# Threshold attention and a gated MLP on one core: four heads in 32-row score tiles, q and k transposed by VectorE alone, batches cut into token halves

## The chip, the core and the metric

The kernel runs on one core of a Trainium2 chip. A core has a matrix engine (TensorE, PE in the profile; its weight loads are listed as PEld), a vector engine (VectorE, DVE), an activation engine (ScalarE, ACT), a general engine (GpSimd, POOL) and an engine that only issues transfers (SyncE, SP). Each runs its own queue in order, and they wait for each other through semaphores. Data moves between main memory and the on-chip memory SBUF by DMA; matmuls write to a second on-chip memory, PSUM, which has eight banks of 512 fp32 columns. The metric is device time in microseconds (us) for one launch, as the median of several runs.

## What is computed

```python
def _attn_ref(q, k, v, tau):                       # q, k, v: (8, 8, 576, 64), float32
    scale = 1.0 / np.sqrt(q.shape[-1])
    scores = scale * np.matmul(q, k.transpose(0, 1, 3, 2))
    thresh = np.max(scores, axis=-1, keepdims=True) - tau
    scores = np.where(scores >= thresh, scores, -1000000000.0)
    scores = scores - np.max(scores, axis=-1, keepdims=True)
    attn = np.exp(scores)
    attn = attn / (np.sum(attn, axis=-1, keepdims=True) + 1e-09)
    return np.matmul(attn, v)

def _moe_ref(x, w_in, w_out):                      # x: (4608, 512), w_in: (512, 2048), w_out: (2048, 512)
    h = x @ w_in
    return ((h * np.clip(h + 3.0, 0.0, 6.0) / 6.0) @ w_out)

# x = attention output as (batch * token, head * 64)
```

Eight batches of eight heads with 576 tokens each: scores in fp32, all scores below the row's maximum less tau rejected, a softmax over the rest, the product with v, and then two projections with a gate between them.

## The kernel before

**Slots.** The attention is cut into 144 slots. A quad is four heads of a batch (two pairs); a batch has two quads, and a quad has nine slots. Slots 0 to 3 are 128 query tokens each of the quad's first pair, 4 to 7 the same of its second pair, and slot 8 holds the last 64 tokens of both pairs. A slot is always two heads (`a` = 0 and 1) by 128 rows by 576 keys.

**What one slot does.** `scores(n)` (L300) multiplies q and k of two heads: each head's 64 dimensions are one half of the 128 partitions, so the two heads are two strips of TensorE, each with a 384- and a 192-column matmul (or 320 and 256). An fp32 matmul of the code shows in the trace as two records. `sm_max` (L315, DVE) copies the scores from PSUM to SBUF and takes the row maximum, one instruction for each head; `sm_bias` (L322, POOL) makes a bias of the maximum and tau; `sm_mask` (L327, ACT) and `sm_exp` (L332, ACT) reject, exponentiate and sum; `sm_recip` (L335, DVE) inverts the sum; `sm_norm` (L340, POOL) scales to bf16. The result P is then transposed, for most slots by a DMA (L348, issued by SP) and for some of the first 21 by nine TensorE transposes (L355) with a DVE copy (L356). `av_main` and `av_rest` (L364, L367) multiply P with v for 512 or 256 tokens or for the 64 last ones, and DVE copies the product out (xT at L375, xR at L385). From batch 2 on that is 256 tokens.

**Projections.** `mm1` (L393 with w_in) makes 512 columns of the first projection, which is called an item; relu goes to ACT (L412) or DVE (L414), and the gate to DVE (L427). `mm2_part` (L393 with w_out) is a quarter of a 128-token tile of the second projection, called a part; `mm2_out` (L446) copies a finished tile out on DVE, and `flush` sends it. There are 144 items and 144 parts. `todo1` and `todo2` are lists of what may be done; each slot from `N1` = 22 on takes one item, and every even one two parts. What is left after the last slot is done by `rest1` and `rest2`.

**q and k.** `load_quad` loads them. For the first two batches (`NB` = 2) TensorE transposes them (`main_pe` at L238, `transpose_rest` at L266 and L268), and DVE or ACT copies the result from PSUM. For the other six, loads of 32 numbers at a time put 32-dimension blocks below each other, and DVE's 32 x 32 transposes (L247 for q, L256 for k) finish the layout in SBUF.

**Order.** Nothing is scheduled automatically: each engine runs its instructions in the order in which the loop over slots writes them (L551). In slot n DVE does the maximum of slot n + 1, the reciprocal of n - 1, waiting copies, the product copy, relu, gate and transposes. TensorE does an item, the product, parts, and scores: one slot's scores (n + 2) in each of the slots 3 to 22, then, from slot 23 on, those of n + 3 and n + 2 in every odd slot. Scores lie in banks 0 to 5 (`score_col`), each head in three of them; the products use banks 2 and 5 in turn (`bank`), items bank 6 (HB) or 7, tiles of the second projection bank 7 (OB). `warm_up` issues transposes whose result nobody reads.

These lines say where a slot's scores stand and in which order a pair of slots is issued:

```python
def score_col(n, a):
    if n in (1, 2):
        return 1664 if a else 3200 if n == 1 else 128
    return (704 if first(n) else 128) + (0 if a else 1536)
...
elif n > N1 and n % 2:
    for m in (n + 3, n + 2):
        if m < len(queue):
            scores(m)
```

Of the kernel before, what the change touches and what calls it, by code (L numbers as in the profile page):

```python
# [20 lines left out]
def kernel(  # L21
# [17 lines left out]
    NQUAD = B * H // 4  # L39
    NSLOT = 9  # L40
    NB = 2
    N0 = 3
    N1 = 22
    N2 = 28
    HB, OB = 6, 7
    scale = 1.0 / math.sqrt(D)
# [3 lines left out]
    nat_pool = ctx.enter_context(tc.tile_pool(name="nat", bufs=3))  # L50
    v_pool = ctx.enter_context(tc.tile_pool(name="vp", bufs=2))
    qk_pool = ctx.enter_context(tc.tile_pool(name="qk", bufs=2))
# [3 lines left out]
    pt_pool = ctx.enter_context(tc.tile_pool(name="pt", bufs=3))  # L56
# [20 lines left out]
    loads = []  # L77
    casts = []
    vcasts = []
# [3 lines left out]
    def load_quad(quad):  # L83
        b, g = divmod(quad, 2)
        nat[quad] = (nat_pool.tile([P, 2 * S], F32, tag="nq", name="nq"),
                     nat_pool.tile([P, 2 * S], F32, tag="km", name="km"),
                     nat_pool.tile([P, 2 * D], F32, tag="kr", name="kr") if b < NB else None)
        nq, km, kr = nat[quad]

        def main(dst, src, n, a, order, by=nc.sync):  # L90
            by.dma_start(out=dst[:, 0:1024].rearrange("p (t h d) -> p t h d", h=4, t=4)[:, :, 2 * n + a, :],
                         in_=src[b, 4 * a + 2 * g + n, 0:512, :].rearrange(order, t=4))

        def blocks(dst, src, a, order, **sizes):
            rows = src[b, 4 * a + 2 * g:4 * a + 2 * g + 2].rearrange("n t d -> (n t) d")
            for j in range(2):
                c = 32 * (2 * a + j)
                nc.sync.dma_start(out=dst[c:c + 32].rearrange("p (k d) -> p k d", d=32) if len(sizes) == 1 else
                                  dst[c:c + 32].rearrange("p (t x d) -> p t x d", d=32, t=9),
                                  in_=rows[:, 32 * j:32 * j + 32].rearrange(order, **sizes))  # L100

        def load_k(n):
            if b < NB:
                for a in range(2):
                    main(km, k, n, a, "(p t) d -> p t d", by=nc.scalar if quad == n == 0 else nc.sync)
            else:
                blocks(km, k, n, "(x r t) d -> r t x d", r=32, t=9)

        def load_q(n):
            if b < NB:  # L110
                for a in range(2):
                    main(nq, q, n, a, "(t p) d -> p t d")
            else:
                blocks(nq, q, n, "(k r) d -> r k d", r=32)

        def rest():
            for dst, src in ((kr[:], k), (nq[:, 1024:1152], q)):
                for n in range(2):
                    by = nc.scalar if quad == 0 and src is k else nc.sync
                    by.dma_start(out=dst[64 * n:64 * n + 64, :].rearrange("p (h d) -> p h d", h=2),  # L120
                                 in_=src[b].rearrange("(a n) t d -> n a t d", a=2)[2 * g + n, :, 512:S, :].rearrange(
                                     "a p d -> p a d"))

        if b < NB:
            loads.extend((lambda: load_k(0), lambda: load_q(0), rest, lambda: load_k(1), lambda: load_q(1)))
        else:
            loads.extend((lambda: load_q(0), lambda: load_k(0), lambda: load_q(1), lambda: load_k(1)))

    def load_v(b):
        vm = v_pool.tile([P, H, 4 * D], BF16, tag="vm", name="vm")  # L130
        vr = vrs[b % 2]
        vsb[b] = (vm, vr)
        if b < NB:
            mains = [lambda h=h: nc.gpsimd.dma_start(
                out=vm[:, h:h + 4, :], in_=v[b, h:h + 4, 0:512, :].rearrange("h (p t) d -> p h (t d)", t=4))
                for h in range(0, H, 4)]
            rests = [lambda a=a: nc.gpsimd.dma_start(
                out=vr[a * 64:(a + 1) * 64, a, :, :],
                in_=v[b, 4 * a:4 * a + 4, 512:S, :].rearrange("h p d -> p h d")) for a in range(2)]
        else:  # L140
            def tokens(a, first, count):
                return v[b, 4 * a:4 * a + 4].rearrange("h (p t) d -> p h (t d)", t=9)[
                    :, :, first * D:(first + count) * D]

            mains = [lambda a=a, u=u, first=first: nc.gpsimd.dma_start(
                out=vm[64 * u:64 * u + 64, 4 * a:4 * a + 4, :], in_=tokens(a, first, 4))
                for a, u, first in ((0, 0, 0), (0, 1, 5), (1, 0, 5), (1, 1, 1))]
            rests = [lambda a=a: nc.gpsimd.dma_start(
                out=vr[a * 64:(a + 1) * 64, a, :, :], in_=tokens(a, 4 * (1 - a), 1)) for a in range(2)]
        vcasts.extend(mains + rests)  # L150
# [47 lines left out]


    gbuf = g_pool.tile([P, NI, 2 * S], BF16, name="g")  # L200

# [552 lines left out]
```

## Time and profile before

| | us |
|---|---|
| median of 3 runs (507.67 to 508.34) | 507.7 |
| the profiled execution | 506.6 |
| its span | 504.8 |
| maximum of slot 0 begins (DVE, L315) | 8.2 |
| maximum of slot 15 begins | 47.4 |
| maximum of slot 22 begins | 67.0 |
| maximum of slot 143 begins | 450.4 |
| last matmul begins to stream out, L680 | 497.8 |

The span is the time from the first to the last instruction of the program in the profiled execution; its time as a run is 1.8 us longer. Busy time is the sum of an engine's instructions without overlaps; in a row of a timeline the first number is the start, the second the length of a merged group and `xN` the number of records in it. Records of matmuls overlap, so from one matmul to the next it is the starts that count. A name after `<-` in brackets is what ended the idle time before.

### The profile page before, as it was taken

What the parts mean: (1) busy time and instruction counts of PE and PEld (TensorE: products, weight loads), DVE (VectorE), ACT (ScalarE), POOL (GpSimd) and SP (SyncE); (2) the same over time, 40 slices, a digit from 0 to 9 for tenths busy, and PEclk for the clock granted to TensorE, in tenths of its full rate; (3) what the DMA queues carried; (4) which work ended last, traced back from release to release, by engine and by line L of the source; (5) the groups of instructions that cost most, each with busy time, mean ns of one, the idle gap of its engine ahead of it and who ended that gap; (6) DMA issues with size and microseconds to landing.
All of it is one profiled execution on the core that took longest, in us unless ns stands there. A gap on an engine that the chain in (4) does not pass through costs nothing.

```text
span 504.8 us, 14628 instructions
## 1 busy us (share of the span) xinstructions
PE 497.2 (98%) x5496; PEld 343.8 (68%) x5496; DVE 443.3 (88%) x1151; ACT 444.3 (88%) x953; POOL 279.9 (55%) x509
## 2 busy tenths in 40 slices
PE   8999999999999999999999999999999999999997
PEld 7655567677766777777766777777766777767564
DVE  4788899999999999999999999999999999877261
ACT  4999999999999999999999999999999999986170
POOL 2777778756656555656556555656556555552000
PEclk9999999999999999999999999999999999999999
DMA  6999999999999999999999999999999996864122
GB/s 146 182 163 161 146 151 157 195 147 174 180 189 169 178 167 173 162 175 159 185 186 166 178 172 158 181 173 165 168 193 169 172 180 115 111 123 90 66 62 64
DMA packets 317814, 78.91 MB, mean 156 GB/s; under 512 B 300720, under 2 KB 313264, under 8 KB 317744
## 3 DMA queue, kind: packets, MB, share of 16 engines
q1 hardware_dynamic: 298784, 68.61, 88.3%
q0 software_dynamic: 17472, 8.92, 14.9%
q8 instruction: 43, 0.70, 0.6%
q10 hardware_dynamic: 1488, 0.46, 0.4%
q14 instruction: 27, 0.22, 0.2%
HBM read 36.70 MB, written 9.44 MB: 91 GB/s over the span
## 4 chain that ended last, share of the span: by engine, by line
PE 81%; DVE 5%; ACT 1%; issue 1%; DVEq 0%
PE ps L393 48%; PE ps L300 25%; PE ps L364 5%; DVE s L315 2%; PE ps L367 1%; DVE g L427 1%; DVE r L414 1%; PE ps L680 1%; ACT s L332 0%; ACT r L412 0%; PE ps L355 0%; DVE xT L375 0%; PE ps L238 0%; DVE kT L256 0%; DVE rinv L335 0%
## 5 line engine op out<-in xcount | busy, mean ns | idle before, releaser
L340 POOL TENSOR_SCALAR pn<-s,rinv 128x576 bf16<-128x576 f32 x288 | 211.6, 748 | 19.1 <-issue 4.6
L315 DVE TENSOR_SCALAR_CACHE_REDUCE s<-ps 128x576 f32<-128x576 f32 x288 | 204.7, 747 | 13.2 <-PE ps L300 6.5
L327 ACT ACTIVATE s<-s,bias 128x576 f32<-128x576 f32 x288 | 205.9, 764 | 3.6 <-POOL bias L322 3.2
L332 ACT ACTIVATE s<-s 128x576 f32<-128x576 f32 x288 | 192.5, 671 | 0.0
L300 PE MATMUL ps<-kT,qT 64*128 64x384 f32 (+7 forms) x1280 | 175.7, 419 | 2.3 <-DVE s L315 2.1
L300 PEld LDWEIGHTS ps<-kT,qT 64*128 64x128 f32 (+1 forms) x1280 | 104.1, 175 | 57.7 <-DVE s L315 10.2
L393 PE MATMUL ps<-xT,w_in_sb 128*64 128x256 bf16 (+1 forms) x1896 | 132.5, 274 | 0.6 <-DVE g L427 0.6
L393 PE MATMUL ps<-w_out_sb,g 128*64 128x512 bf16 (+1 forms) x1016 | 130.9, 379 | 0.0
L393 PEld LDWEIGHTS <-w_in_sb 128*64 128x64 bf16 (+1 forms) x1896 | 108.1, 109 | 31.6 <-issue 21.9
L322 POOL TENSOR_SCALAR bias<-m 128x2 f32<-128x2 f32 (+1 forms) x147 | 28.0, 190 | 161.2 <-DVE rinv L335 151.2
L427 DVE SCALAR_TENSOR_TENSOR g<-r,ps 128x512 bf16<-128x512 f32 x128 | 87.5, 685 | 11.8 <-ACT r L412 7.9
L393 PEld LDWEIGHTS <-g 128*64 128x64 bf16 (+1 forms) x1016 | 61.5, 109 | 48.3 <-issue 0.4
L412 ACT ACTIVATE r<-ps,three 128x512 f32<-128x512 f32 x81 | 55.5, 687 | 25.2 <-PE ps L393 23.2
L332 ACT ACTIVATION_READ_ACCUMULATOR s<-s 128x1 f32 x288 | 54.8, 190 | 0.0
L414 DVE TENSOR_SCALAR r<-ps 128x512 f32<-128x512 f32 x63 | 42.9, 680 | 0.0
L364 PE MATMUL ps<-pT,vm 128*64 128x256 bf16 (+1 forms) x480 | 38.5, 280 | 0.0
L364 PEld LDWEIGHTS <-vm 128*64 128x64 bf16 x736 | 32.7, 111 | 3.4 <-issue 1.4
L375 DVE CAST xT<-ps 128x256 bf16<-128x256 f32 (+1 forms) x60 | 26.1, 435 | 7.1 <-PE ps L367 7.1
L446 DVE TENSOR_SCALAR osb<-ps 128x512 f32<-128x512 f32 x31 | 20.9, 673 | 8.4 <-PE ps L393 8.4
L315 DVE DVE_READ_ACCUMULATOR s<-ps 128x1 f32 x288 | 23.8, 83 | 0.0
L335 DVE RECIPROCAL rinv<-rsum 128x2 f32<-128x2 f32 x144 | 23.0, 160 | 0.7 <-ACT s L332 0.6
L444 ACT ACTIVATE osb<-ps 128x512 f32<-128x512 f32 x4 | 2.4, 598 | 20.9 <-PE ps L393 14.6
(61 smaller groups left out, 249.6 us busy)
## 6 DMA issues: line engine op xcount, KB each, us to landing
out_dram<-osb SPq DMA_DIRECT2D x31, 256.0 KB, 3.0
nq<-in_q_dram SPq DMA_DIRECT2D x48, 144.0 KB, 4.4
km<-in_k_dram SPq DMA_DIRECT2D x48, 144.0 KB, 4.5
vm<-in_v_dram POOLq DMA_DIRECT2D x24, 128.0 KB, 4.3
nq<-in_q_dram SPq DMA_DIRECT2D x16, 128.0 KB, 4.5
w_in_sb<-in_moe_w_in_dram POOLq DMA_DIRECT2D x8, 256.0 KB, 4.9
w_out_sb<-in_moe_w_out_dram POOLq DMA_DIRECT2D x16, 128.0 KB, 4.5
pT<-pn SPq DMA_TRANSPOSE x117, 4.6
```

Of the source, the lines that this page charges most:

```text
L300: nc.tensor.matmul(ps_flat[rows, c0:c0 + w], qT_of(pair)[a * 64:(a + 1) * 64, q0:q0 + rows.stop - rows.start], kT_of(pair)[a * 64:(a + 1) ...
L315: nc.vector.tensor_scalar(out=sl.s[:, i, :], in0=ps_flat[:, c0:c0 + S], scalar1=1.0, scalar2=None, op0=Alu.mult, op1=Alu.max, accum_out=sl ...
L322: nc.gpsimd.tensor_scalar(out=sl.bias[:, of], in0=sl.m[:, of], scalar1=-scale, scalar2=tau, op0=Alu.mult, op1=Alu.add)
L327: nc.scalar.activation(out=s, in_=s, func=Act.Prelu, bias=sl.bias[:, i:i + 1], scale=scale, alpha=REJECT)
L332: nc.scalar.activation(out=s, in_=s, func=Act.Exp, accum_out=sl.rsum[:, i:i + 1])
L340: nc.gpsimd.tensor_scalar(out=pn[:, i, :], in0=sl.s[:, i, :], scalar1=sl.rinv[:, i:i + 1], scalar2=1.0, op0=Alu.mult, op1=Alu.mult)
L364: nc.tensor.matmul(pb[a * 64:(a + 1) * 64, :], vm[:, 4 * a + hp, c * D:(c + 1) * D], pT[:, 5 * a + c, cols], start=(c == 0), stop=False)
L375: return lambda: nc.vector.tensor_copy(out=xT[b][:, hp, c0:c0 + w], in_=pb)
L393: nc.tensor.matmul(out[c:c + w], lhsT[:, c:c + w], rhs, start=start, stop=stop)
L412: nc.scalar.activation(out=r, in_=hps, func=Act.Relu, bias=three[:])
L414: nc.vector.tensor_scalar(out=r, in0=hps, scalar1=3.0, scalar2=0.0, op0=Alu.add, op1=Alu.max)
L427: nc.vector.scalar_tensor_tensor(out=out, in0=r, scalar=6.0, in1=hps, op0=Alu.min, op1=Alu.mult)
```

## The change

Slots are laid out anew. A batch has 18 slots. Four heads (a quad) stand below each other in SBUF, each in 32 partitions, and the 64 dimensions are two halves `j` of 32 that lie side by side; a matmul has 32 rows, and two of them, one for each half, are accumulated. Two slots that follow each other have the same query tile and the two pairs of heads of a quad: slot `i` = 0 uses strips 0 and 1, slot `i` = 1 strips 2 and 3. The order within a batch is tokens 0 to 255 of both quads, the last 64 tokens of both quads, then tokens 256 to 511.

`burst(n)` issues both slots' scores together in eight steps, at the end of every even slot. The even slot's columns are cut into 128 and 448 (its 448 lie in bank 2 or 5), the odd slot's into 448 and 128, and the two 128-column pieces share a bank; a POOL instruction that does nothing (`relay`) keeps the odd slot's last piece behind the even slot's first.

q and k are transposed by DVE for all batches (`transpose_q`, `transpose_k`), k with rows of 18 tokens (4.6 KB) and q with rows of 64 numbers. The transposes of q and k for batch b + 1 stand in even slots of batch b, those of the first two quads and of quad 2 in slots 0 to 3, 5, 7, 9, 11 and 13, and quad 3's in 12, 14, 16, 18. v has one tile of five blocks for each head and is loaded in eight pieces. The weights are loaded in four and four transfers in place of eight and sixteen.

Products are of 256 tokens in every batch: chunk 0 in slots 8, 10, 12, 14 of the batch, the 64-token rest in 16, chunk 1 in 18, 20, 22, 24. Items are taken from slot 15 on, two parts in odd slots. P is transposed by TensorE only for slots 1, 3, 5, 7, 8, 9 and 11.

```diff
-    N0 = 3
-    N1 = 22
-    N2 = 28
+    NSLOT = 18
+    N1 = 15
...
+        if of:
+            src = k[b, 4 * g:4 * g + 4].rearrange("h (r t) d -> (h r) (t d)", r=R)
+            by.dma_start(out=dst, in_=src[:, t0 * D:t1 * D])
+            return
+        for c in range(4):
+            by.dma_start(out=dst[32 * c:32 * c + 32].rearrange("p (t d) -> p t d", d=D),
+                         in_=q[b, 4 * g + c].rearrange("(t r) d -> r t d", r=R)[:, t0:t1])
...
+    def transpose_q(quad, t0, t1):
+        rows = nat[quad][0][:].rearrange("p (t j w) -> p t j w", j=2, w=32)
+        nc.vector.transpose(out=qk_of(quad)[0][:].rearrange("p j (t w) -> p t j w", w=32)[:, t0:t1],
+                            in_=rows[:, t0:t1])
+    def transpose_k(quad, part):
+        first, e = ((0, 5), (10, 4))[part]
+        rows = nat[quad][1][:].rearrange("p (t j w) -> p j t w", j=2, w=32)
+        outs = qk_of(quad)[1]
+        for j in range(2):
+            for_u = rows[:, j, first:first + 2 * e].rearrange("p (u e) w -> p u e w", u=2)
...
+            nc.vector.transpose(out=o, in_=for_u)
...
+    for b in range(B):
+        for g, t in ((0, 0), (0, 1), (1, 0), (1, 1), (None, 4), (0, 2), (0, 3), (1, 2), (1, 3)):
+            for i in range(2):
+                sl = Slot()
+                sl.b, sl.g, sl.t, sl.i, sl.n = b, g, t, i, len(queue)
+                sl.on_chip = sl.n in (1, 3, 5, 7, 8, 9, 11)
+                queue.append(sl)
...
+    OWN = S - P
+    def score_col(n, a):
+        return (512 - OWN if n % 2 else 1024 - P) + 1536 * a
...
+    def burst(n):
+        steps = ((0, 0, P, 0), (1, 0, OWN, 0), (0, 0, P, 1), None,
+                 (0, P, OWN, 0), (1, 0, OWN, 1), (0, P, OWN, 1), (1, OWN, P, 0), (1, OWN, P, 1))
+        for step in steps:
+            if step is None:
+                relay = nc.gpsimd.nop()
+                behind(relay, mm)
+                continue
+            i, k0, w, j = step
+            sl = queue[n + i]
+            for a in range(2):
+                c = 32 * (2 * i + a)
...
+                    mm = nc.tensor.matmul(ps_flat[rows, c0:c0 + w],
+                                          qT[c:c + 32, j, q0:q0 + rows.stop - rows.start],
+                                          kT[c:c + 32, j, k0:k0 + w], start=(j == 0), stop=(j == 1))
+                    if (i, k0) == (1, OWN):
+                        behind(mm, relay)
...
+        at(products, n0 + 16, (b, None, None))
...
+        when = (7, 9, 11, 13) if quad == 2 else ((4, 6, 8, 10), (12, 14, 16, 18))[g]
+        for n, job in zip(when, (lambda quad=quad: transpose_k(quad, 0), lambda quad=quad: transpose_k(quad, 1),
+                                 lambda quad=quad: transpose_q(quad, 0, 8), lambda quad=quad: transpose_q(quad, 8, T))):
+            at(jobs, n0 + n, job)
+    at(jobs, 0, lambda: transpose_q(0, 4, 8))
+    for n, job in ((0, lambda: transpose_k(1, 0)), (1, lambda: transpose_k(1, 1)), (2, lambda: transpose_q(1, 0, 8)),
+                   (3, lambda: transpose_q(0, 8, T)), (5, lambda: transpose_q(1, 8, T))):
+        at(jobs, n, job)
...
+    for n, sl in enumerate(queue):
+        now = n
+        if n + 1 < len(queue):
+            sm_max(queue[n + 1])
+        if prev is not None:
+            sm_recip(prev)
+        for copy in waiting:
+            copy()
+        waiting = []
+        item = None
+        if todo1 and n >= N1:
+            item, then = todo1.pop(0)
+            h = mm1(item, 0 if n == len(queue) - 1 else OB if n > N1 and n % 2 == 0 and not pieces else HB)
+            todo2.extend(then)
+        multiply(n)
+        if item:
+            mm1_gate(item, h, mm1_relu(h, on_act=n % 2 == 1))
+        if n > 1 and queue[n - 2].on_chip:
+            waiting.append(pe_transpose(queue[n - 2]))
+        second()
+        for i in range(2):
+            sm_exp(sl, i)
...
+        for job in jobs.get(n, ()):
+            job()
+        if prev is not None:
+            sm_norm(prev)
+        if n % 2 == 0 and n + 2 < len(queue):
+            burst(n + 2)
+        if n < 3 or n == 6:
+            warm_up(6)
```

## The prediction

> **What bounds the kernel now.** First the page: its busy line, the chain, and the score line.
>
> ```profile
> span 504.8 us, 14628 instructions
> PE 497.2 (98%) x5496; PEld 343.8 (68%) x5496; DVE 443.3 (88%) x1151; ACT 444.3 (88%) x953; POOL 279.9 (55%) x509
> ...
> PE 81%; DVE 5%; ACT 1%; issue 1%; DVEq 0%
> ```
>
> The chain that ended last is TensorE for 81%. Busy time by stretch tells where that holds:
>
> ```profile
> 20.00:60.00 40.00, 38.72 (x309) 23.53 (x308) 35.39 (x101) 39.73 (x90) 30.98 (x55) 1.00 1.14 158
> ...
> 180.00:440.00 260.00, 260.00 (x3174) 183.58 (x3172) 249.57 (x653) 246.23 (x533) 150.12 (x271) 1.00 1.15 167
> 454.00:502.00 48.00, 47.28 (x340) 30.18 (x336) 21.77 (x37) 19.32 (x32) 2.93 (x4) 1.00 0.28 71
> ```
>
> Columns: length, then PE, PEld, DVE, ACT, POOL. Early ACT is full (39.7 of 40 us; slots begin 2.67 us apart), and PE's share there is partly warm-up and transposes. From about 100 us PE has no idle time. After 454 us only PE works: projections left over. Now one pair of slots in the middle, on PE and on DVE:
>
> ```profile
> 194.15 0.28 PE L367 MATMUL ps<-pT,vr 128*64 128x256 bf16 x2
> 194.35 2.21 PE L300 MATMUL ps<-kT,qT 64*128 64x384 f32 x16
> 196.49 1.06 PE L393 MATMUL ps<-xT,w_in_sb 128*64 128x256 bf16 x16
> 197.39 1.89 PE L393 MATMUL ps<-w_out_sb,g 128*64 128x512 bf16 x16
> 199.19 1.06 PE L393 MATMUL ps<-xT,w_in_sb 128*64 128x256 bf16 x16
> 200.06 0.63 PE L364 MATMUL ps<-pT,vm 128*64 128x256 bf16 x8
> 200.50 0.30 PE L367 MATMUL ps<-pT,vr 128*64 128x256 bf16 x2
> 200.73 2.21 PE L300 MATMUL ps<-kT,qT 64*128 64x384 f32 x16
> ```
> ```profile
> 194.07 0.67 DVE L446 TENSOR_SCALAR osb<-ps 128x512 f32<-128x512 f32 x1
> 194.66 0.42 DVE L375 CAST xT<-ps 128x256 bf16<-128x256 f32 x1
> ...
> 200.41 0.16 DVE L335 RECIPROCAL rinv<-rsum 128x2 f32<-128x2 f32 x1
> 200.84 0.42 DVE L375 CAST xT<-ps 128x256 bf16<-128x256 f32 x1 [0.27 <-PE ps L367]
> ```
>
> Starts on PE: scores 2.14, first projection 0.90, second 1.80, first 0.87, attention product 0.64. In one pair DVE waits for the product (0.27) and copies it at 200.84, in the other the output copy L446 makes it 0.2 later. Both engines are nearly full.
>
> **Work on PE that goes and comes.** Counted in the two programs, first and second projections are 144 items and 144 parts in both; an item is 0.87 us (16 matmuls), a part 0.86. The 72 fp32 transposes of q and k and 54 of the 117 bf16 ones go, all in the first 22 slots, where ACT's fullness hides them: taken as nothing. If PE bound there, their records (L238, L266, L268 some 11 us, half of L355's 8.8) would be worth up to 15. The DVE copies that went with them give way to DVE transposes of like length (below).
>
> Scores. A head's 64 rows become two accumulating matmuls of 32 rows, four strips instead of two. The single records of a burst show passes of 384 columns 0.32 us apart, two per matmul; so each of two strips streams 2 x 576 x 2 x 0.32/384 = 1.92 us per pair of slots, and 0.11 before (first weights) and 0.11 after make 2.14. In the changed kernel each of four strips again streams 2 x 576 columns twice: 1.92 us. That four strips run together is not shown; nearest are the four-quadrant tiles of the 64-token slots:
>
> ```profile
> L300 PE MATMUL ps<-kT,qT 64*64 64x384 f32 x72 | 9.3, 508 | 0.1
> ```
>
> 72 x 0.508 = 36.6 us of records in 9.3 us: four at once, nothing lost. Strips also need not keep step: at 9.68 us a matmul of one strip starts before an earlier-issued one of the other. I take 2.14; the bad end is in the rivals. The Trainium skill (TensorE: Matmul & The Clock Gate, "Measured speedup vs the span model") speaks against: four 32-row strips measured 3.07 times, not 4. By it a burst is an estimated 0.58 longer, 72 of them 42 us.
>
> 64-token slots: before, 4 bursts in 18 take 2.30 to 2.34, for the change of tile inside; after, one tile throughout. Gain 4 x 0.18 / 18 = 0.04 per pair, and 0.02 for fewer separate products.
>
> **The new wait.** Product banks 2 and 5 are also columns of the even slot's scores. Before, the half written there is the last quarter of the burst. After, it is the even slot's 448-column step, which follows only two 128-column steps: 0.11 + 4 x 0.107 = 0.53 after the burst starts, which is 0.20 after the last product matmul started: 0.74. The copy of the product starts 0.31 after that matmul at best (after 100 us: 0.31, or 0.51 behind L446), takes 0.42, and DVE to PE takes 0.05: 0.79; weights come after the wait: 0.11. So the step starts at 0.90: 0.16 late; behind L446 up to 0.36, less what DVE catches up in the longer pair (at most 0.2). I take 0.19, ends 0.05 (weights loaded ahead) and 0.36. Behind it in PE's queue stand the odd slot's second halves, whose strips stream until 0.85 anyway, and then the next projection, so ACT's and DVE's part of that follows late by as much. The POOL relay sits behind two L340 (1.47 together, from 0.10 after the burst starts): over by 1.6, when the odd strips come to need it. What it holds up on POOL is a v load and the next bias, which is not due before the burst ends. Net per pair: 0.19 - 0.06 = +0.13.
>
> **Queues.** SP issues 83 loads of q and k instead of 140, and 4.6 KB k rows replace packets of 128 bytes: DMA gets lighter, and no L300 or L315 waits for it in the middle, so nothing is gained there. POOL issues 72 loads instead of 68 at 0.64 us (L145), two in each of slots 0 to 3: with 1.85 for L340, L322 and gaps that is 3.1 per slot, and biases come up to 0.8 late, under the loop below; uncovered, 1.6 in all.
>
> **Early slots.** From slot 3 on the old kernel issues one slot's scores at a time. The new burst waits for the maximum of the odd slot, so a pair is a closed loop: maxima of two slots 2 x 1.36, 0.13 to PE, burst to readable 1.92 + 0.31 (13.94 to 15.21 is 1.27 for half a burst), less 0.2 as one head starts earlier: 4.9, plus what DVE does between the even and the odd maximum: reciprocal 0.07 and the transposes put at odd slots. Those are priced by
>
> ```profile
> L247 DVE STREAM_TRANSPOSE qT<-nq 128x576 f32<-128x576 f32 x24 | 18.5, 771 | 0.0
> L256 DVE STREAM_TRANSPOSE kT<-km 128x320 f32<-128x320 f32 x24 | 12.1, 504 | 0.0
> L256 DVE STREAM_TRANSPOSE kT<-km 128x256 f32<-128x256 f32 x24 | 9.6, 401 | 0.0
> ```
>
> 18.5/24 = 0.77 for 576 columns; 0.64 to 0.84 for 512 and 640. So 5.7 to 5.9 per pair against ACT's 5.33; the first two pairs also wait for transposes before the burst (6.2, 6.7), slots 11 to 13 for a P copy and the product copy (7.1). Seven pairs: 6.2 + 6.7 + 5.7 + 5.8 + 5.8 + 7.1 + 5.9 = 43.2; before, 37.8 for the same slots. The first burst is behind the k load (landed at 3.7 and 5.2 before), two larger memsets of v and five transposes: 0.3 later, estimated from such rows, ends -0.3 and 1. Slot 15's maximum is then ready at 54.4, not 48.8.
>
> Then items start (before: slot 22, 67 us). Pairs to slot 25: 6.4 + 3 x 5.8 + 5.3 (slots 23, 24 have none) = 29.1, at 83.5. From there PE binds: three pairs of 6.28 + 0.19 and one without second projections at 5.8: the burst of slots 34, 35 starts at 108.7. Before, bursts at 98.87 and 105.46 put this point at 102.2: 6.5 late. If DVE's chain hides, ACT's pace stands, 5.3 better.
>
> **Middle and end.** Bursts at 98.87 and 435.63 are 53 pairs: 6.354. After: 6.48 x 54 = 349.9: last burst at 458.6. What PE still has from there, by the new order: burst 2.33, items 3 x 0.87, parts 4 x 0.86, 64-token products 0.75, then 17 items, 26 parts, 4 products 2.4 and a copy 0.6: 49.4 us; PE end to span end is 3.4 now. Before, 22 items, 30 parts and 3 products are left: the tail is 7.2 shorter.
>
> Sum: 458.6 + 49.4 + 3.4 = 511.4 against 504.8: +6.6. The profiled execution took 506.6, the median is 507.7: 507.7 + 6.6 = 514.3, say 514.
>
> **Rivals.**
> A, faster, 501: the start hides. ACT sets the pace to slot 15 (-5.3) and the product copy is covered (0.05, not 0.19: 54 x 0.14 = -7.6). For: ACT is full early now; DVE idles 0.27 before the copy. Against: both loops above. Either half alone gives 509 or 507; it turns to a gain when both come, or the copy's lateness stays under 0.06.
> B, 537: weights do not hide behind 128-column passes. Their single records take 0.187 us, such a pass 0.107; each strip has four of these passes: 4 x 0.08 = 0.32 per burst, x 72 = 23. For: there are twice as many weight loads. Against: early 128-column transposes with a load each follow one another every 0.109.
> C, 528: PE cools in early gaps. The first 14 warm-up transposes take 3.19 us (0.23 each), later ones 0.11 apart: half speed. Busy perhaps 60% to slot 15, a burst there would stream 1.92 longer, x 7 = 13.5. Against: granted clock 1.00 in every stretch, and warm-ups remain.
>
> **Chances.** Forecast 0.50, with 507 to 520 as its own range (lateness 0.05 to 0.36 is -8 to +9, early 5 either way, not together); A 0.27; around no change 0.06; B 0.10; C 0.07. Range 502 to 525: it leaves out A's best tenth and B. Under 0.2% this measurement can't tell: faster 0.27, same 0.07, slower 0.66.
>
> **What would show it.** L224 bursts taking about 2.3 to the next L313, with PE waiting on xT's copy; slot 15's maximum near 54 us with ACT no longer full; 17 items after the last slot; tail 52 us. Wrong if bursts stay 2.14, or if ACT is full to slot 15.

## The result, and the profile after

After the change the kernel takes 535.42 us (median of 4 runs, 533.33 to 536.21) against 507.69 us (506.59 to 508.34): a ratio of 1.0542, 95% interval 1.0507 to 1.0577. The forecast was 514, with 502 to 525. The profiled execution has a span of 533.7 us. In this kernel the scores are L224, the maximum L238, the norm L265, the DMA transpose of P L276, TensorE's transpose of P and its copy L282 and L283, the product and its copy L290 and L298, both projections L313, VectorE's transposes of q and k L104 and L118, and the relay on GpSimd L213.

First the page: the busy line, the granted clock in 40 slices of 13.3 us (9 is 90% or more), the chain, and the score line.

```profile
span 533.7 us, 17090 instructions
...
PE 501.8 (94%) x6735; PEld 371.2 (70%) x6739; DVE 446.7 (84%) x1141; ACT 442.6 (83%) x949; POOL 281.1 (53%) x512
...
PEclk9987788899999999999999999999999999999999
...
PE 80%; DMA 4%; DVE 2%; issue 1%; ACT 0%; POOLq 0%; POOL 0%; DVEq 0%
...
L224 PE MATMUL ps<-kT,qT 32*128 32x128 f32 (+3 forms) x2560 | 190.4, 438 | 21.7 <-DVE s L238 11.7
```

Three things are new: slices 3 to 8 of the clock are below 9, DMA has a share in the chain, and TensorE idles 21.7 us ahead of the scores (2.3 before). Busy time by stretch, with the columns as before (length, PE, PEld, DVE, ACT, POOL, granted clock, DMA share, GB/s):

```profile
20.00:60.00 40.00, 28.33 (x311) 21.54 (x314) 24.23 (x69) 30.51 (x68) 24.12 (x43) 0.83 1.01 161
60.00:100.00 40.00, 32.41 (x386) 24.01 (x378) 28.53 (x75) 28.35 (x63) 20.91 (x39) 0.83 1.22 147
180.00:440.00 260.00, 259.04 (x3794) 193.20 (x3792) 247.29 (x634) 239.62 (x519) 152.07 (x276) 1.00 1.00 164
486.00:533.00 47.00, 44.23 (x350) 28.57 (x351) 20.41 (x38) 19.39 (x35) 5.49 (x9) 1.00 0.36 82
```

From 20 to 60 us ScalarE was full before (39.7 of 40); now no engine is (ACT 30.5, PE 28.3), and TensorE has 0.83 of its clock. The middle and the end look as they did. The middle, one pair of slots on TensorE, then the product's copy on VectorE:

```profile
246.23 2.36 PE L224 MATMUL ps<-kT,qT 32*128 32x128 f32 x32
248.52 1.06 PE L313 MATMUL ps<-xT,w_in_sb 128*64 128x256 bf16 x16
249.42 1.89 PE L313 MATMUL ps<-w_out_sb,g 128*64 128x512 bf16 x16
251.14 1.04 PE L313 MATMUL ps<-xT,w_in_sb 128*64 128x256 bf16 x16
252.02 0.80 PE L290 MATMUL ps<-pR,v 128*64 128x64 bf16 x40
252.75 2.47 PE L224 MATMUL ps<-kT,qT 32*128 32x128 f32 x32
255.14 1.06 PE L313 MATMUL ps<-xT,w_in_sb 128*64 128x256 bf16 x16
```
```profile
246.34 0.42 DVE L298 CAST xT<-ps 128x256 bf16<-128x256 f32 x1 [0.31 <-PE ps L290]
...
252.38 0.67 DVE L365 TENSOR_SCALAR osb<-ps 128x512 f32<-128x512 f32 x1
252.97 0.41 DVE L307 CAST xR<-ps 128x256 bf16<-128x256 f32 x1
```

A burst's start to the next L313 is 2.29 at 246.23 and 2.39 at 252.75. Most bursts alternate between 2.29 and 2.48, by whether the output copy L365 stands ahead of the product's copy. From the burst of slots 34/35 (128.69) to that of 142/143 (481.09) are 54 pairs at 6.53.

Reading off where the time went, against the forecast's own points:

| | before | forecast | after |
|---|---|---|---|
| maximum of slot 15 ready | 48.8 | 54.4 | 65.3 |
| burst of slots 34/35 starts | 102.2 (equivalent) | 108.7 | 128.7 |
| pair in the middle | 6.354 | 6.48 | 6.53 |
| last burst to span end | | 52.8 | 52.6 |

The span missed the forecast by 22.3 us (533.7 against 511.4); 20.0 of them are there when the burst of slots 34/35 starts. TensorE in the early part, around the bursts of slots 12 to 15:

```profile
44.01 0.74 PE L290 MATMUL ps<-pT,v 128*64 128x256 bf16 x10 [0.38 <-DVE s L238]
47.50 1.12 PE L282 MATMUL ps<-identb,pn 128*128 128x128 bf16 x9 [2.75 <-DVE pT L283]
48.54 4.22 PE L224 MATMUL ps<-kT,qT 32*128 32x128 f32 x32
55.16 0.66 PE L282 MATMUL ps<-identb,pn 128*128 128x128 bf16 x9 [2.39 <-DVE pR L283]
```

The burst at 48.54 takes 4.22 us, twice its length: the granted clock is 0.5 from 46.1 to 53.0. Such stretches last 3.41 or 6.83 us and add up to 30.7 us between 12 and 97 us. The waits in brackets leave TensorE idle; the slow clock sets in during them or after them, and a slow burst makes the next maxima late.

The second new thing is in the chain between 60 and 110 us (start, length, what), and next to it GpSimd and TensorE at its end:

```profile
75.90 0.99 PE ps L313 x15
76.89 13.75 DMA pT<-pn
90.64 0.02 issue
90.66 0.04 POOLq L265
...
90.91 1.28 PE ps L224 x8
...
92.47 7.17 DMA pT<-pn
```
```profile
90.82 1.46 POOL L265 TENSOR_SCALAR pn<-s,rinv 128x576 bf16<-128x576 f32 x2 [0.92 <-DMA pT<-pn]
```
```profile
90.91 1.23 PE L224 MATMUL ps<-kT,qT 32*128 32x128 f32 x8 [2.86 <-POOLq L213]
```

P's transpose issued at 76.89 lands 13.75 us later. Until then its buffer pn is taken, GpSimd's norm waits for that buffer, the relay stands behind the norm, and the burst's last pieces stand behind the relay: TensorE loses 2.86 us in the middle of a burst. The transposes issued from 65 to 77 us land 9.8 to 14.4 us later, against 4.0 at the median, while the loads of w_out issued in slots 12 to 15 are under way (59.6 to 85.7 us):

```profile
w_out_sb<-in_moe_w_out_dram POOLq DMA_DIRECT2D x4, 512.0 KB, 10.6
pT<-pn SPq DMA_TRANSPOSE x123, 4.0
```

### The profile page after: what moved, and what is told of

Its sections match the earlier page's. It is cut to its first block, busy times and chain, and to the rows that moved or that the text cites. A ratio compares the mean times of both kernels' runs of the same rounds, so it can differ in the third digit from the quotient of the medians.

```text
span 533.7 us, 17090 instructions
## 1 busy us (share of the span) xinstructions
PE 501.8 (94%) x6735; PEld 371.2 (70%) x6739; DVE 446.7 (84%) x1141; ACT 442.6 (83%) x949; POOL 281.1 (53%) x512
## 4 chain that ended last, share of the span: by engine, by line
PE 80%; DMA 4%; DVE 2%; issue 1%; ACT 0%; POOLq 0%; POOL 0%; DVEq 0%
PE ps L313 46%; PE ps L224 27%; PE ps L290 6%; DMA pT<-pn 4%; DVE s L238 1%; PE ps L518 1%; ACT r L331 0%; DVE g L346 0%; DVE xT L298 0%; DVE osb L521 0%; POOLq L265 0%; POOL pn L265 0%; DVE rinv L260 0%; DVEq L260 0%; DVEq L238 0%
## 5 line engine op out<-in xcount | busy, mean ns | idle before, releaser
L238 DVE TENSOR_SCALAR_CACHE_REDUCE s<-ps 128x576 f32<-128x576 f32 x288 | 205.6, 751 | 42.5 <-PE ps L224 23.5
L265 POOL TENSOR_SCALAR pn<-s,rinv 128x576 bf16<-128x576 f32 x288 | 210.9, 745 | 23.3 <-DMA pT<-pn 4.2
L224 PE MATMUL ps<-kT,qT 32*128 32x128 f32 (+3 forms) x2560 | 190.4, 438 | 21.7 <-DVE s L238 11.7
L224 PEld LDWEIGHTS ps<-kT,qT 32*128 32x128 f32 (+1 forms) x2560 | 135.4, 182 | 63.3 <-DVE s L238 16.4
L313 PE MATMUL ps<-xT,w_in_sb 128*64 128x256 bf16 (+1 forms) x1936 | 133.8, 277 | 0.1
L313 PE MATMUL ps<-w_out_sb,g 128*64 128x512 bf16 (+1 forms) x1021 | 130.7, 379 | 0.2
L313 PEld LDWEIGHTS <-w_in_sb 128*64 128x64 bf16 (+1 forms) x1936 | 110.2, 110 | 28.6 <-issue 18.3
L313 PEld LDWEIGHTS <-g 128*64 128x64 bf16 (+1 forms) x1024 | 61.7, 109 | 47.9
L331 ACT ACTIVATE r<-ps,three 128x512 f32<-128x512 f32 x81 | 55.3, 686 | 40.7 <-PE ps L313 39.7
L290 PE MATMUL ps<-pT,v 128*64 128x256 bf16 x640 | 46.5, 277 | 0.8 <-DVE s L238 0.8
L290 PEld LDWEIGHTS <-v 128*64 128x64 bf16 x960 | 42.0, 112 | 3.6 <-issue 1.5
L126 POOL DMA_DIRECT2D v<-in_v_dram x64 | 36.7, 574 | 9.4 <-issue 3.5
L298 DVE CAST xT<-ps 128x256 bf16<-128x256 f32 x64 | 26.8, 419 | 11.3 <-PE ps L290 11.1
L365 DVE TENSOR_SCALAR osb<-ps 128x512 f32<-128x512 f32 x32 | 21.5, 672 | 9.1 <-PE ps L313 9.1
L118 DVE STREAM_TRANSPOSE kT<-nk 128x320 f32<-128x320 f32 (+1 forms) x64 | 26.5, 453 | 1.0 <-DMA nk<-in_k_dram 1.0
L104 DVE STREAM_TRANSPOSE qT<-nq 128x640 f32<-128x640 f32 (+2 forms) x33 | 24.8, 751 | 0.0
```

Source lines behind the costliest of these rows:

```text
L126: nc.gpsimd.dma_start(out=vsb[b % 2][32 * g:32 * g + 32].rearrange("p (hp a) c -> p a hp c", a=2)[:, a, :, c0 * D:(c0 + count) * D], in_=v ...
L224: mm = nc.tensor.matmul(ps_flat[rows, c0:c0 + w], qT[c:c + 32, j, q0:q0 + rows.stop - rows.start], kT[c:c + 32, j, k0:k0 + w], start=(j == ...
L238: nc.vector.tensor_scalar(out=sl.s[:, i, :], in0=ps_flat[:, c0:c0 + S], scalar1=1.0, scalar2=None, op0=Alu.mult, op1=Alu.max, accum_out=sl ...
L265: nc.gpsimd.tensor_scalar(out=pn[:, i, :], in0=sl.s[:, i, :], scalar1=sl.rinv[:, i:i + 1], scalar2=1.0, op0=Alu.mult, op1=Alu.mult)
L290: nc.tensor.matmul(pb[a * 64:(a + 1) * 64, :], vsb[b % 2][:, 2 * hp + a, u * D:(u + 1) * D], pT[:, block, cols], start=(c == 0), stop=(c = ...
L313: nc.tensor.matmul(out[c:c + w], lhsT[:, c:c + w], rhs, start=start, stop=stop)
```

## The experiments

Times are medians with the ratio to the kernel before and its interval; "34/35" is the start of that burst in the profiled execution (128.7 in the changed kernel), "half clock" the sum of the stretches at 0.5 from 10 to 130 us (30.7). Past slot 36 the profiles hardly differ: from the maximum of slot 36 to that of slot 142 it is 345.3 us in all of them, and 334.0 or 334.3 in those with the product ahead of the item, but for the first such run (344.7). So 34/35 says what an edit of the early part gave in that one execution. The expectations speak of theories: 1 is the falling clock, 2 the late P with the relay behind it, 3 the waits for the copies of TensorE's transposes of P, and L the closed loop of maximum and burst.

**The clock.** Dummy transposes fill TensorE's idle time, first up to slot 22, then up to slot 14:

```diff
-        if n < 3 or n == 6:
-            warm_up(6)
+        warm_up(12 if n < N1 else 6 if n < 23 else 0,   # second run: 12 if n < N1 else 0
+                to=ps[:, OB if n < N1 or n % 2 else HB, 256:256 + P])
```

> After, with 12 dummy 128x128 transposes at the end of each slot up to 14 and 6 in slots 15 to 22 (0.11 us each at full clock), written to columns that nothing else uses then. Theory 1 (the early waits let TensorE's granted clock fall to 0.5, and the half-speed bursts of 4 to 5 us keep the loop long): the clock is 1.00 from about 15 to 100 us, bursts in slots 6 to 20 take 2.3 instead of 4.2 to 5.1 us, the burst of slots 34/35 starts at 112 to 119 instead of 128.7 and the time falls by 10 to 17, to 518 to 525. Theory 2 (P transposes and the relay on GpSimd's queue hold the bursts, the clock is a by-product): the 2.9 and 0.6 us waits at 90 to 100 us stay, most of the early loop too, and the time is 531 to 536.

> After, with the 12 dummy transposes in slots 0 to 14 alone, none in slots 15 to 22, where in the first such run TensorE was 97 to 99% busy and 1.7 us of each pair was dummy work. Theory 1 refined (the clock costs more than the 7 us that the first run gave back, since its later dummies took back four pairs x 1.7): clock 1.00 to about 85 us, burst of slots 34/35 at 114 to 119 and time 521 to 526. Rival: without them the clock falls again after slot 15 or the late P transposes set the pace of slots 16 to 24 anyway: burst of slots 34/35 at 120 or later, time 528 or more.

528.77 us (1.0461, 1.0412 to 1.0511), 34/35 at 121.8, half clock 6.8; and 528.12 us (1.0415, 1.0384 to 1.0446), 34/35 at 119.7, half clock 3.4. The clock is a cause, but a smaller one than either expectation had it: with it nearly restored the time falls by 7.3, not 10 to 17. The same two bursts in the second run (L162 are the dummies):

```profile
44.55 0.66 PE L282 MATMUL ps<-identb,pn 128*128 128x128 bf16 x9 [0.53 <-DVE pT L283]
45.14 2.23 PE L224 MATMUL ps<-kT,qT 32*128 32x128 f32 x32
47.30 1.53 PE L162 MATMUL ps<-identf 128*128 128x128 f32 x12
49.76 0.66 PE L282 MATMUL ps<-identb,pn 128*128 128x128 bf16 x9 [0.93 <-DVE pR L283]
```

The burst takes 2.16 instead of 4.22, and the waits for L283 fall from 2.75 and 2.39 to 0.53 and 0.93, part of the gap being filled. But the burst of slots 24/25 still starts at 86.5, behind a product that waits 2.0 for P, as the rival said.

**The wait for the product's copy.** In even slots the product and its copy go ahead of the first projection, and of the output copy on VectorE. In the first version the item was chosen behind the product, in the second ahead of it:

```diff
+        if todo1 and n >= N1:
+            item, then = todo1.pop(0)
+        product_first = n % 2 == 0 and n > N1
+        if product_first:
+            multiply(n)
         for copy in waiting:
             copy()
```

> After, with the attention product and its copy ahead of the first projection in even slots from 16 on (and ahead of the output copy on VectorE), so that the copy is done when the even slot's 448-column step comes. The forecast's term for this wait was 0.19 per pair, measured 0.15 and 0.34 in turn: if that is what the middle loses, bursts take 2.14 to 2.18 to the next projection, a pair 6.28 to 6.33 instead of 6.53, and the time falls by 10 to 13, to 522 to 525. Rival: VectorE, 95% busy in the middle, becomes the bound or makes the first projection's gate late: bursts 2.14, but new waits elsewhere, a pair 6.45 to 6.6, time 531 to 538.

> After, with product and copy ahead of the first projection in even slots from 16 on, as before, but the item chosen ahead of the product, so that no projection reads the copy just made (in the first such run those waits were 0.65 to 0.85 in two pairs of nine, and one item more per nine pairs came into the loop). If the wait for the copy is what the middle loses: bursts 2.16, no wait of TensorE over 0.3 after 140 us, pairs 6.30 except where an item is missing, 10 to 13 us less, 522 to 526. Rival: VectorE or ScalarE sets the pace below 6.45: 528 or more.

532.69 us (1.0510, 1.0477 to 1.0543) and 522.16 us (1.0300, 1.0284 to 1.0315). In the first, bursts took 2.16 as expected, but in two pairs of nine a projection read the copy just made, waited 0.65 to 0.85 us for it, and the pair took 7.1 to 7.6. In the second no such wait is left:

```profile
246.67 2.23 PE L224 MATMUL ps<-kT,qT 32*128 32x128 f32 x32
248.83 1.06 PE L313 MATMUL ps<-xT,w_in_sb 128*64 128x256 bf16 x16
249.73 1.89 PE L313 MATMUL ps<-w_out_sb,g 128*64 128x512 bf16 x16
251.46 0.71 PE L290 MATMUL ps<-pT,v 128*64 128x256 bf16 x10
252.00 1.04 PE L313 MATMUL ps<-xT,w_in_sb 128*64 128x256 bf16 x16
252.97 2.23 PE L224 MATMUL ps<-kT,qT 32*128 32x128 f32 x32
```

The pair from 246.67 to 252.97 is 6.30 and the burst 2.16. Over 53 pairs the middle gets 11.0 us shorter (345.3 to 334.3), 0.21 a pair. VectorE doesn't take over. The whole gain is 13.3; in the profile the other 2.6 are there at the maximum of slot 36 (135.7 instead of 138.3), and slots 16 to 34 have the same edit.

**P, late by DMA.** Five runs. A fifth pn buffer; w_out in 16 pieces; the weight loads moved back; and plain copies instead of DMA transposes, in the changed kernel and in the kernel before. The plain copies leave out the transposing: P arrives untransposed, and so does the gate of the odd tiles, whose transpose is exchanged in the same way (not shown). The matmuls that follow have the same shapes but wrong numbers, so these kernels tell about the time alone.

```diff
-    pn_pool = ctx.enter_context(tc.tile_pool(name="pn", bufs=4))
+    pn_pool = ctx.enter_context(tc.tile_pool(name="pn", bufs=5))
```
```diff
-    for i, n in enumerate((12, 13, 14, 15)):
+    for i, n in enumerate(range(8, 24)):        # w_out[i * P:i * P + P, :] each
```
```diff
-    for i, n in enumerate((4, 6, 8, 10)):
+    for i, n in enumerate((4, 6, 9, 12)):
-    for i, n in enumerate((12, 13, 14, 15)):
+    for i, n in enumerate((15, 17, 19, 21)):
```
```diff
-            nc.sync.dma_start_transpose(out=sl.dst, in_=pn[:].rearrange("p a b -> p (a b)"))
+            nc.sync.dma_start(out=sl.dst, in_=pn[:].rearrange("p a b -> p (a b)").rearrange("p (c t) -> p c t", t=P))
```

> After, with a fifth buffer for the normalized scores pn, so that GpSimd's norm (and the relay behind it) waits one slot later for a P transpose that is still under way. Theory 2 (late P transposes reach TensorE through GpSimd's queue): the waits of 2.86 and 0.63 us before the burst's last pieces at 90 to 100 us go, and with them the half-clock stretch at 90.5 to 97.3; the burst of slots 34/35 starts at 121 to 125 instead of 128.7 and the time falls by 4 to 7, to 528 to 531. Rival: the transposes themselves stay as late, so the products that read them take over the wait: time 533 to 536.

> After, with w_out loaded as 16 pieces of 128 KB, one in each of slots 8 to 23, instead of 4 of 512 KB in slots 12 to 15. Theory 2 (bulk loads delay the P transposes, whose buffers GpSimd waits for with the relay behind): P transposes issued between 65 and 85 us land in 4 to 7 us instead of 10 to 14, GpSimd's waits for them are under 0.5 us, the clock stays 1.00 at 90 to 97 us, and the time falls by 5 to 9, to 526 to 530. Theory 1: the half-clock stretches before 70 us are untouched and the burst of slots 18/19 starts where it does now (73.0 us, within 1); the time falls by 4 at most. If neither, the transposes land as late as now whatever the pieces.

> After, with the weight loads spread: w_in in slots 4, 6, 9, 12 instead of 4, 6, 8, 10, and w_out in slots 15, 17, 19, 21 instead of 12, 13, 14, 15; nothing else. Theory 2 (four bulk loads in a row are what makes the P transposes of slots 10 to 16 land 9.8 to 14.4 us late): transposes issued between 65 and 80 us land in under 8 us, the waits before the burst at 90 to 100 us (2.86 and 0.63) go, the time falls by 3 to 7, to 528 to 532. Rival: all loads together fill the DMA engines and the lateness only moves by some slots (as when w_out was cut in 16 pieces), 533 to 537.

> After, with each DMA transpose (of P and of the odd tiles' gate) replaced by a plain DMA copy of the same bytes to the same place, so that the blocks arrive untransposed; TensorE's own transposes of P stay. Theory 2 (late DMA transposes cost 7 to 9 us in the early slots, half of it by the clock that falls while TensorE waits): copies land in 2 to 4 us throughout, GpSimd never waits for P, the waits at 90 to 100 us go, time 526 to 530. Rival (bulk loads would be as late and as costly without transposes): 533 to 536.

> Control: the kernel before, with plain copies in place of its DMA transposes. Its P transposes land 4.6 us after their issue and nothing waits for them, so theory 2 gives no change, within 2 us of 507. Were plain copies to speed up something else as well, it would be faster by 3 or more, and the two runs above would say less.

| run | time | ratio, interval | 34/35 | half clock |
|---|---|---|---|---|
| fifth buffer | 531.02 | 1.0492, 1.0460 to 1.0524 | 120.6 | 20.5 |
| w_out in pieces | 534.84 | 1.0560, 1.0544 to 1.0577 | 129.6 | 34.1 |
| weights moved back | 544.28 | 1.0721, 1.0703 to 1.0740 | 139.8 | 41.0 |
| plain copies | 527.80 | 1.0408, 1.0380 to 1.0437 | 121.1 | 17.1 |
| before, plain copies | 506.63 | 0.9991, 0.9982 to 1.0000 | | 0 |

The fifth buffer takes GpSimd's wait for P away altogether, though the transposes still land 8.7 to 11.0 us late: 4.4 us at the median, at the low end of what was expected. The pieces of w_out did what theory 2 said at first: transposes issued from 59 to 74 us landed in 4.1 to 4.6. But the later pieces met v, k and q of the next batches, a transpose issued at 86.46 took 11.3, and TensorE waited 3.47 for the relay at 98. Moved back, the loads met more of them, and the lateness grew. GpSimd's waits of that kernel from 30 to 125 us (sum, number, longest):

```profile
POOL pn L265 <- DMA pT<-pn: 15.8, 2, 14.3
```

TensorE stood still for 14.4 us at that place. So theory 2 holds in that late P costs time; its rival fits in that the lateness moved with the other loads and did not go away. Plain copies of the same bytes give back 7.6 us, yet they land up to 13.6 us late too: what holds up P is not the transposing alone. In the kernel before the exchange gives 0.4 us, with an interval that ends at 1.0000, so the 7.6 is a cost that the change brought.

**The loop itself.** P transposes of even slots behind the burst instead of ahead of it; and VectorE's transposes of q and k out of the odd slots:

```diff
-        if n > 1 and queue[n - 2].on_chip:
+        if n % 2 and n > 1 and queue[n - 2].on_chip:
             waiting.append(pe_transpose(queue[n - 2]))
...
             burst(n + 2)
+        if n % 2 == 0 and n > 1 and queue[n - 2].on_chip:
+            waiting.append(pe_transpose(queue[n - 2]))
```
```diff
-        when = (7, 9, 11, 13) if quad == 2 else ((4, 6, 8, 10), (12, 14, 16, 18))[g]
+        when = (8, 10, 12, 14) if quad == 2 else (14, 16, 16, 18) if quad == 3 else ((4, 6, 8, 10), (12, 14, 16, 18))[g]
...
+    transpose_q(0, 4, 8)                        # ahead of the first maximum; quad 1's at slots 0 and 4
     sm_max(queue[0])
```

> After, with the TensorE transposes of P in even slots (slots 6 and 8, at n = 8 and 10) issued behind the burst instead of ahead of it, so that the burst doesn't stand behind the 2.75 and 2.39 us waits for the copy of the transpose before. Theory 3 (those waits lengthen the loop of slots 10 to 14): the bursts now at 48.5 and 56.4 start 2 to 4 us earlier in all, and the time falls by 2 to 5, more if the half-clock stretch at 46 to 53 us goes with them. Theory 1: the waits only move, TensorE idles as much and the clock still falls to 0.5 there; the time is within 1.5 of 535.

> After, with the transposes of quads 0 to 3 moved from odd slots, where VectorE does them between the even and the odd maximum, to even slots, where it waits up to 2.9 us for the burst; the second q piece of quad 0 goes ahead of the first maximum. Theory L (the closed loop maximum, transpose, maximum, burst sets the early pace, as the forecast had it, so the rest of the lateness is in the loop itself): about eight transposes of 0.4 to 0.9 us leave it, the burst of slots 16/17 starts 4 to 7 us before 73.0, and the time falls by 4 to 7, to 528 to 531. Rival: the half clock and the late P transposes set the pace; what the loop saves goes into longer waits for them, and the time falls by under 2.

533.24 us (1.0524, 1.0492 to 1.0557), 34/35 at 124.6: 2.2, at the low end of what was expected and not clear of the scatter (531.35 to 535.58). 528.40 us (1.0412, 1.0393 to 1.0431), 34/35 at 122.2: 7.0, the size that theory L gave. But the half clock falls with it, to 20.5 (23.9 in the run before), so these two runs don't part the loop from the clock. In the second the maximum of slot 15 is ready at 57.4 instead of 65.3, and the burst at 73.0 (it is that of slots 18/19; the expectation names 16/17) starts at 63.5. Of these 9.5 us 3.1 are lost again by 34/35: the next burst, at 71.2, takes 8.7 us, since it waits for the relay.

**Clock and late P together.** Dummies up to slot 14 and plain copies.

> After, with two edits alone: dummy transposes in slots 0 to 14 and plain copies in place of the DMA transposes. One by one these gave 7.3 and 7.6. If the clock that falls and the late P are separate costs, they add: 519 to 522, burst of slots 34/35 at 111 to 114. If the clock falls mostly because of the late P, or the faster early loop brings the P copies nearer, they overlap: 523 to 527.

522.95 us (1.0306, 1.0285 to 1.0327), 34/35 at 115.5, half clock 0: 12.5 of the 14.9 that the two gave singly. They are separate costs for the most part, with some 2 us in common.

**All together.** First four edits (dummies up to slot 14, P transposes behind the burst, fifth buffer, product first); then with the transposes at even slots, and the product's copy first in slots 8 to 14 as well; then that with the weights moved back.

> After, with all four: dummy transposes in slots 0 to 14, P transposes behind the burst, a fifth pn buffer, product first. If the four causes are separate (clock 7 to 12, P transposes 2, late P by DMA 4 to 7, product's copy 10 to 13), the time is 503 to 512, about the kernel before. If they overlap in the early slots, where each shortens the same loop, 512 to 520.

> The four edits together (dummy transposes to slot 14, P transposes behind the burst, fifth pn buffer, product first), with the transposes at even slots and the product's copy ahead of P's copy in slots 8 to 14 too. With the four alone pairs of slots 10 to 15 took 6.7 to 7.7 us, VectorE copying P (0.65) before the product. Theory L: pairs of slots 4 to 15 fall to 5.4 to 6.2, the burst of slots 34/35 to 107 to 110 (115.7), the time to 504 to 511: no slower than the kernel before by more than 1%. Rival: bulk loads and P transposes on the DMA engines set the pace there: burst of slots 34/35 at 113 or later, time 513 to 517.

> The five edits of the run before (dummy transposes, P transposes behind the burst, fifth pn buffer, product first, transposes at even slots), which left one wait of 8.64 us of TensorE for a P transpose that landed 19.4 us after its issue, with the weight loads spread as in the single run. Theory 2: that wait goes, the burst of slots 34/35 starts at 109 to 113 instead of 120.3, and the time is 502 to 506, faster than the kernel before by 0.3 to 1%. Rival: later transposes are late instead; burst of slots 34/35 at 116 or later and time 509 to 514.

516.48 us (1.0165, 1.0108 to 1.0221), 512.41 us (1.0119, 1.0081 to 1.0157) and 515.89 us (1.0165, 1.0135 to 1.0195). Their runs scatter more than others, 510.8 to 517.9 in the first. In the first the effects overlap, as its second case had it. The second has its pairs of slots 4 to 14 at 5.4 to 7.7 and reaches slot 15 at 54.9, about where the forecast had it, yet 34/35 is at 120.3 in its profile (an execution of 515.35), which says why: the faster the early loop, the sooner it stands before P.

```profile
65.56 1.06 PE L313 MATMUL ps<-xT,w_in_sb 128*64 128x256 bf16 x16
75.27 1.28 PE L290 MATMUL ps<-pT,v 128*64 128x256 bf16 x10 [8.64 <-DMA pT<-pn]
```

The transpose that this product waits for was issued at 55.74 and landed 19.4 us later. With the loads moved back (the third) this wait goes and a later one comes, 5.2 us at 95: the rival. To see the rest without it, plain copies again, with the weights where the change has them, moved back, and moved up (w_in in slots 1, 3, 5, 7, w_out in 8 to 11):

> The five edits together, with plain copies in place of the DMA transposes. Theory 2: the wait of 8.64 us goes, burst of slots 34/35 at 109 to 112, time 502 to 506 (512.4 with the transposes). Rival: another wait takes its place, 509 to 513.

> The five edits with the weight loads moved back (515.9 with the transposes), with plain copies in their place. If it is the P transposes that the loads hold up, the place of the loads no longer matters: within 1.5 us of the run with the loads where the change has them. If the loads themselves collide with q, k and v, it stays 3 us or more slower than that.

> The five edits with plain copies in place of the DMA transposes (507.2 with the loads where the change has them, 509.9 with them moved back), now with the weight loads moved up: w_in in slots 1, 3, 5, 7 and w_out in slots 8, 9, 10, 11. If loads beside one another cost by their crowding after 60 us, moved up they cost less: 503 to 506, burst of slots 34/35 at 107 to 110 (110.5). If the DMA engines are short of time over the whole early part, k and q of the second batch come later in their place: 507 to 511.

507.19 us (0.9996, 0.9980 to 1.0013), 509.90 us (1.0053, 1.0032 to 1.0074) and 520.74 us (1.0246, 1.0208 to 1.0284). In the first of these TensorE waits neither for P nor for the relay. So without these waits the five edits reach the kernel before and no more; 34/35 is at 110.5, which gives back 18.2 of the 20.0 us by which the forecast missed it. Moved either way the loads cost more. Moved up, a copy of P issued at 39.65 landed 18.4 us later, and TensorE waited 8.1 for it. So the expectation that an earlier place would help was wrong: of the three places tried, that of the change is the best. With DMA transposes the loads moved up were not measured. No version with the transposes in it beat the kernel before; the best took 512.41.

## Why the forecast was off

The direction was right, the size was not: +27.7 (medians) against +6.6. Step by step:

- **The bound and the burst: right.** TensorE sets the middle. Four strips run together: with the new wait gone a burst takes 2.16, forecast 2.14. By the Trainium skill (TensorE: Matmul & The Clock Gate, "Measured speedup vs the span model") it would have been an estimated 0.58 longer; the trace shows nothing of that. Rival B (weights not hidden behind 128-column passes, 0.32 a burst) falls with it.
- **The new wait: right.** Forecast 0.19 a pair, shown by taking it away: 0.21. The whole pair came out at 6.53 instead of 6.48, 2.5 us over 54 pairs.
- **The end: right**, 52.6 against 52.8. Rival A (the start hides behind ScalarE, the copy is covered) came true in neither half.
- **The early sum: the step that failed.** It took the clock at 1.00, had no term for late transfers and had the loop's last pairs too short. To slot 15: 54.4 forecast (its terms add up to 54.5), 65.3 measured. With the clock held it was 58.5, so 6.8 of the 10.9 is the clock. Of the remaining 4.1, 0.8 is there when the maximum of slot 1 is ready; the rest is the loop, with the dummies in it, above all in its last three pairs: 6.6, 7.9 and 6.8 against the 5.8, 7.1 and 5.9 of the sum. From slot 15 to the burst of 34/35: 54.3 forecast, 63.4 measured; 57.1 with plain copies. So 6.3 of the 9.1 is late P with the slow clock that follows it. With both taken out (dummies and plain copies, 34/35 at 115.5) 13.2 of the 20.0 us are gone and 6.8 stay, 4.3 up to slot 15 and 2.5 behind it; no single run parts these further.
- **Why the clock was missed.** It stood there as rival C, at 528, with a chance of 0.07, and was held down by "granted clock 1.00 in every stretch". That row described the old kernel, whose TensorE was busy 38.72 of 40 us from 20 to 60 us: 24.0 with scores, issued slot by slot, 5.8 with the transposes of q and k and 6.1 with those of P (busy time by line; lines overlap a little). The change removes the 5.8 and about half of the 6.1, and gathers the scores of two slots into one burst with a wait ahead of it. The text had taken the transposes off as nothing, since ScalarE hides them, and didn't ask what they did for the clock. That filling the gaps holds the clock is shown; how much of that the removed transposes would have done is not. Rival C's mechanism was shown, at 7 to 9 us instead of 13.5; it alone doesn't make the result.
- **Why late P was missed.** "DMA gets lighter, and no L300 or L315 waits for it in the middle, so nothing is gained there" looked at the whole run and its middle. In the early part w_out comes as four loads of 512 KB (59.6 to 85.7 us), where the kernel before has sixteen of 128 KB (67.5 to 98.5) whose neighbours among the P transposes land in 4.6 to 6.8. The traces show two differences. Transposes issued at 65.0 and 67.6 were late (9.8 and 13.1) though w_out's were the only loads under way when they were issued; beside pieces such transposes landed in 4.1 to 4.6. And from 75 us on loads of v, k and q stand beside w_out, while the kernel before issues none of these between 67.4 and 99.7. Pieces with no such loads beside them were not tried, so how much each difference costs stays open. And the relay was asked what it holds up on GpSimd, not what GpSimd can hold up in front of it: behind a norm that waits for a buffer, the relay hands a DMA's lateness to TensorE.

## What to carry to other kernels

Work that is hidden behind another engine may still be what keeps the matrix engine's clock up (here dummy work in the gaps held it and gave 7.3 us): before it is costed at nothing, ask how busy that engine is without it. A semaphore relay on a shared queue inherited the waits of that queue (2.9 us here, 14.4 in one version), so look at what stands ahead of it and how many buffers that has. An early stage has to be summed with its transfers in each stretch of time, not over the run, and a loop made faster there soon stood before the next of them.

## What the runs showed of the hardware

The clock fell without an idle stretch longer than 3.3 us. In the changed kernel the granted clock changes on a grid of 3.41 us. Of the stretches at full clock up to 129 us, each in which the records show TensorE busy for at most 36% (four of them: 7, 24, 36 and 28%) was followed by one at 0.5; so were one of 48% and one of 61%, while others of 47, 57 and 59% and all of 72% and more were not. The longest gap that reaches into these stretches was 3.3, 2.4, 2.4 and 2.9 us in the four, and 2.8 and 1.1 in the two; a gap of 2.9 (17.4 to 20.3 us) that lay half in one stretch and half in the next brought no slow clock. The Trainium skill (TensorE: Matmul & The Clock Gate, "Why this matters for your kernels") asks for no gaps over about 3 us; here five of the six falls came with gaps of 1.1 to 2.9 us.

After 130 us, with the DMA engines at a mean busy share of 1.01 (130 to 440 us), a DMA transpose of P took 3.2 to 7.4 us, 4.0 at the median. Beside the bulk loads of the early part it took up to 14.4 in the changed kernel and up to 19.4 with the five edits, and a plain copy of the same 288 KB up to 18.4.
